# Attention values with the weights as the stationary operand and the sum as one more column

## The chip, the cores and the metric

The kernel runs on one core of one Trainium2 chip. The time is the device time of one execution in microseconds (us), the median of several. Most executions agree within 0.3%. A ratio is the mean time of one kernel's fast runs over that of the other's fast runs of the same rounds, so it is not quite the ratio of the medians quoted beside it.

The engines are called as in the profile: PE is TensorE (matmuls), PEld its weight loads, DVE VectorE, ACT ScalarE, POOL GpSimd (here mostly an issuer of transfers), SP the engine that issues the remaining transfers. L309 is line 309 of that kernel's source, so the same statement has other numbers in other kernels.

## The reference

Attention over keys that are also the values, pooled 4x4 from `kv` and projected, and then a two-layer block with a sigmoid GELU:

```python
kv_pool = kv.reshape(B, H//4, 4, W//4, 4, C).mean(axis=(2, 4))   # B=4, C=128, 768 keys a batch
k = v = kv_pool.reshape(B, -1, C) @ w_sr
s = (q @ k.transpose(0, 2, 1)) / sqrt(C)                          # 12288 queries a batch
a = exp(s - s.max()); a /= a.sum(-1) + 1e-9
x = a @ v
h = x @ w_in                                                      # 128 -> 2048
out = (h * sigmoid(1.702 * h)) @ w_out                            # 2048 -> 128
```

## The kernel before

Queries are taken in 96 groups of 512 tokens (a superset is four groups, a tile 128 tokens); the 768 keys are six chunks of 128. For three (group, chunk) pairs at a time TensorE makes scores, keys on the partitions and tokens on the columns, and ScalarE puts their exponentials in a ring `ag`. The values and sums are drained from the ring later, in an order fixed when the kernel is built: a small scheduler there keeps its own clock and decides what goes between the scores. PSUM's banks 6 and 7 are the two accumulators; the other six hold scores.

```python
def drain_attn(i, jc):                      # values: v stationary, 512 tokens moving
    if jc == 0:
        av_of[i] = acc(("av", i))
    nc.tensor.matmul(av_of[i], vs[b][:, jc, :], weights(("a", i, jc)),
                     start=(jc == 0), stop=(jc == JC - 1))
    if jc == JC - 1:                        # [cut] scale on the way out of PSUM
        nc.vector.tensor_tensor(xs[s][:, ...], av_of.pop(i), rb_of.pop(i), MUL)

def sums(s):                                # per superset: a column of ones times the weights
    ss = acc()
    for jc in range(JC):
        for gi in range(4):
            nc.tensor.matmul(ss[32*gi:32*gi+32, :], ones, weights(("a", 4*s+gi, jc)), ...)
    nc.vector.transpose(t1, ss); nc.vector.reciprocal(col, col); nc.vector.transpose(t2, t1)
    for gi in range(4):
        nc.gpsimd.partition_broadcast(rb, t2[32*gi:32*gi+1, :])

def background(i):                          # what is asked for beside group i
    if i % 4 == 0:
        load_qT(s + 2)                      # SP: transposing load of q for a superset
        cast_q(s + CAST)                    # POOL: q to bf16, HBM to HBM
    if i == 9:
        for jc in range(JC):
            load_chunk(1, jc)               # POOL: batch 1's keys, six casting loads
    # [cut] from group 15 on: pool_chunk, key_chunk, value_chunk of batch 1 on TensorE
```

Batches 2 and 3, which are needed much later, come otherwise: sixteen transfers each that add into SBUF (`add_kv`), then one add of two halves on DVE and transposes on TensorE.

The softmax here doesn't subtract the row's maximum and nothing guards it: scores larger than these inputs give would overflow.

## Time and profile before

| | before |
|---|---|
| time, median | 993.4 us |
| PE busy / ACT busy | 970.8 / 958.4 us of a span of 990.9 |
| DVE / POOL busy | 207.3 / 126.8 us |
| ACT's idle time before the exponentials | 19.6 us (all 196), 15.9 of it before the 188 of full size |

Both PE and ACT are near full. To see which one bounds, one counts each PE instruction at the distance between starts of its kind. That is done in the prediction, which also shows the lines. The same count is used below as "work", and the time from the first matmul to the end of the last less the work is called PE's idle time: 960.8 us of work and 24.4 us idle for the kernel before.

### The profile page before, as it was taken

The numbers are of one execution on the slowest core, as the hardware profiler recorded it, in microseconds if no ns is written. First come the engines' busy times: TensorE is split into PE (matmuls) and PEld (weight loads), VectorE is DVE, ScalarE is ACT, GpSimd is POOL, SyncE is SP. The second block draws the span as 40 slices with busy tenths as digits, with TensorE's granted clock in tenths as the row PEclk, the third lists the DMA queues.
The fourth block names the chain that finished last, engine by engine and source line by source line (L and its number), as shares of the span: only waits on it lengthen the run. The fifth ranks groups of instructions, "written<-read, shape, count | busy, mean of one in ns | idle before, by whom it ended". The sixth has DMA issues, their size and how long they took to land.

```text
span 990.9 us, 13081 instructions
## 1 busy us (share of the span) xinstructions
PE 970.8 (98%) x5041; PEld 438.7 (44%) x5135; DVE 207.3 (21%) x352; ACT 958.4 (97%) x713; POOL 126.8 (13%) x171
## 2 busy tenths in 40 slices
PE   7899999999999999999999999999999999999997
PEld 3444444444444444444444444444444444444443
DVE  4443334211110111101113333430110111011101
ACT  4999999999999999999999999999999999999997
POOL 3221322530133000000002222220000000000000
PEclk9999999999999999999999999999999999999999
DMA  9996941892399322222245520001222221222222
GB/s 182 166 210 113 120 86 33 97 158 43 74 150 173 60 37 41 35 41 43 41 77 97 112 59 22 1 1 32 43 36 40 43 43 33 43 44 39 36 43 43
DMA packets 273663, 69.10 MB, mean 70 GB/s; under 512 B 247552, under 2 KB 271232, under 8 KB 273280
## 3 DMA queue, kind: packets, MB, share of 16 engines
q0 software_dynamic: 29104, 32.51, 21.4%
q1 hardware_dynamic: 243440, 35.61, 21.2%
q8 instruction: 40, 0.66, 0.3%
q10 hardware_dynamic: 1056, 0.13, 0.1%
q14 instruction: 23, 0.19, 0.1%
HBM read 52.49 MB, written 35.65 MB: 89 GB/s over the span
## 4 chain that ended last, share of the span: by engine, by line
PE 87%; ACT 6%; DMA 4%; issue 1%; DVE 1%; POOL 0%; ACTq 0%; POOLq 0%
PE banks L389 31%; PE banks L382 31%; PE banks L312 11%; PE banks L304 11%; ACT ag L384 5%; DMA qT<-q_bf 4%; PE banks L327 3%; ACT ag L306 1%; DMA x<-in_q_dram 1%; DVE qT L209 1%; PE banks L203 0%; DVE o_sb L396 0%; PE banks L157 0%; POOL x L192 0%; PE banks L172 0%
## 5 line engine op out<-in xcount | busy, mean ns | idle before, releaser
L384 ACT ACTIVATE ag<-banks 128x1536 bf16<-128x1536 f32 x512 | 690.8, 1487 | 3.3 <-PE banks L382 2.7
L382 PE MATMUL banks<-x,w_in_sb 128*128 128x512 bf16 x1495 | 408.3, 379 | 1.1
L389 PE MATMUL banks<-ag,w_out_sb 128*128 128x512 bf16 x1510 | 405.3, 379 | 3.0 <-ACT ag L384 0.7
L306 ACT ACTIVATE ag<-banks 128x1536 bf16<-128x1536 f32 (+2 forms) x196 | 261.9, 1454 | 19.6 <-PE banks L304 19.6
L382 PEld LDWEIGHTS <-w_in_sb 128*128 128x128 bf16 x1536 | 149.7, 98 | 183.5 <-issue 6.5
L389 PEld LDWEIGHTS <-w_out_sb 128*128 128x128 bf16 x1536 | 150.0, 98 | 180.4 <-issue 0.8
L396 DVE STREAM_TRANSPOSE o_sb<-banks 128x512 f32<-128x512 f32 x96 | 68.8, 717 | 548.2 <-PE banks L389 521.1
L304 PE MATMUL banks<-qT,kT 128*128 128x512 bf16 x551 | 154.4, 379 | 8.1 <-ACT ag L306 4.5
L312 PE MATMUL banks<-ag,v 128*128 128x512 bf16 x574 | 155.4, 379 | 0.3
L338 POOL PARTITION_BROADCAST rb<-t x96 | 66.6, 797 | 425.7 <-DVE t L335 425.7
L319 DVE TENSOR_TENSOR x<-banks,rb 128x512 bf16<-128x512 f32 x96 | 66.4, 692 | 147.0 <-PE banks L312 124.5
L304 PEld LDWEIGHTS <-kT 128*128 128x128 bf16 x576 | 53.9, 97 | 78.2 <-issue 16.2
L312 PEld LDWEIGHTS <-v 128*128 128x128 bf16 x576 | 55.8, 98 | 66.7 <-issue 0.4
L146 POOL DMA_DIRECT2D kvs<-in_kv_dram x32 | 40.3, 1286 | 97.6 <-DMA kvs<-in_kv_dram 53.0
L327 PE MATMUL banks<-ag,ones 128*32 128x512 bf16 x576 | 35.5, 381 | 0.0
L331 DVE STREAM_TRANSPOSE t<-banks 128x512 f32<-128x512 f32 x24 | 17.2, 717 | 38.5 <-PE banks L327 38.5
L327 PEld LDWEIGHTS <-ones 128*32 128x32 bf16 x576 | 13.2, 96 | 20.6 <-issue 10.2
L335 DVE STREAM_TRANSPOSE t<-t 128x512 f32<-128x512 f32 x24 | 17.1, 711 | 1.0
L180 POOL DMA_DIRECT2D q_bf<-in_q_dram x20 | 10.9, 578 | 8.6 <-DMA x<-in_kv_dram 6.3
L209 DVE COPY qT<-banks 128x512 bf16<-128x512 bf16 x15 | 9.6, 686 | 3.7 <-PE banks L203 3.5
L250 PE MATMUL banks<-ones 128*32 128x512 bf16 x19 | 7.3, 513 | 0.9 <-DVE col L228 0.9
L123 PEld LDWEIGHTS <-x 128*128 128x128 bf16 x192 | 6.5, 96 | 3.0 <-DMA x<-in_kv_dram 0.5
(48 smaller groups left out, 82.4 us busy)
## 6 DMA issues: line engine op xcount, KB each, us to landing
out_dram<-o_sb SPq DMA_DIRECT2D x382, 64.0 KB, 1.9
kvs<-in_kv_dram POOLq DMA_DIRECT2D x32, 384.0 KB, 6.5
q_bf<-in_q_dram POOLq DMA_DIRECT2D x20, 512.0 KB, 7.5
x<-in_kv_dram POOLq DMA_DIRECT2D x12, 512.0 KB, 12.7
x<-in_q_dram POOLq DMA_DIRECT2D x3, 512.0 KB, 20.1
w_in_sb<-in_moe_w_in_dram POOLq DMA_DIRECT2D x1, 512.0 KB, 5.3
w_out_sb<-in_moe_w_out_dram POOLq DMA_DIRECT2D x1, 512.0 KB, 12.9
x<-in_q_dram POOLq DMA_DIRECT2D x1, 384.0 KB, 7.0
```

Source lines behind the costliest of these rows:

```text
L146: nc.gpsimd.dma_start(out=kv_sums[b][:, i2], in_=kv_p[b, i, w, :, i2], **({"accum_op": ADD} if n else {}))
L209: nc.vector.tensor_copy(dst, src)
L304: nc.tensor.matmul(ps[:, k, :], kTs[i // GB][:, jc * 128:(jc + 1) * 128], rhs, start=True, stop=True)
L306: nc.scalar.activation(place([("a",) + c for c in chunks]), ps, AF.Exp, scale=scale)
L312: nc.tensor.matmul(av_of[i], vs[b][:, jc, :], weights(("a", i, jc)), start=(jc == 0), stop=(jc == JC - 1))
L319: nc.vector.tensor_tensor(xs[s][:, (i % 4) * G:(i % 4 + 1) * G], av_of.pop(i), rb_of.pop(i), MUL)
L327: nc.tensor.matmul(ss[32 * gi:32 * gi + 32, :], ones, weights(("a", 4 * s + gi, jc)), start=(jc == 0), stop=(jc == JC - 1))
L338: nc.gpsimd.partition_broadcast(rb, t2[32 * gi:32 * gi + 1, :])
L382: nc.tensor.matmul(ps[:, k, :], w_in_sb[:, fc * 128:(fc + 1) * 128], xs[g // 4][:, (g % 4) * G:(g % 4 + 1) * G], start=True, stop=True)
L384: nc.scalar.activation(place([("m",) + c for c in chunks]), ps, AF.Gelu_apprx_sigmoid)
L389: nc.tensor.matmul(o_of[g], w_out_sb[:, fc, :], weights(("m", g, fc)), start=(fc == 0), stop=(fc == FCH - 1))
L396: nc.vector.transpose(o_sb, o_of.pop(g))
```

## The change

Its intent: with the weights stationary and the values moving, the result has tokens on the partitions. A 129th column of ones in the values then gives each token its sum beside its values, so that the block of sums, its two transposes on DVE and the four broadcasts on POOL fall away, and the scaling is by one number a partition. The price is four times as many weight loads, and six transposes on PE per six tiles, to bring the result back to tokens on columns.

```diff
-        nc.tensor.matmul(av_of[i], vs[b][:, jc, :], weights(("a", i, jc)), ...)
-    def sums(s): ...                                   # and its broadcasts
+    def drain_attn(t, a):                              # tile t of 128 tokens, half a of the chunks
+        for jc in range(a * K, a * K + K):
+            nc.tensor.matmul(av_of[u][:, k*(C+1):(k+1)*(C+1)], weights(("a", i, jc))[:, o:o+T],
+                             vs[i // GB][:, jc, 0:C+1], start=(jc == 0), stop=(jc == JC - 1))
+        if k == TS - 1 and a == 1:                     # three tiles fill an accumulator
+            nc.vector.reciprocal(rec, ps[:, :, C])
+            nc.vector.tensor_tensor(xt, ps[:, :, 0:C], rec.unsqueeze(2).broadcast_to(...), MUL)
+    def turn(w):                                       # six tiles back
+        for k in range(6):
+            nc.tensor.transpose(ps[:, k, :], xt[:, k, :], ident)
+        nc.vector.tensor_copy(x[:, o:o + 6 * T], ps)
 ... background(i):
-        if i == 9:
-            for jc in range(JC):
-                load_chunk(1, jc)
-        ... pool_chunk, key_chunk, value_chunk of batch 1
+        if i in ADDS:                                  # [4, 6, 8, 9, 11, 12, 14, 15]
+            add_kv(1, ADDS.index(i))                   # two accumulating transfers each
+        if i in (17, 19):
+            use_kv(1, (i - 17) // 2)                   # DVE adds halves, PE transposes
-    AG = 99
+    AG = 108
```

The last part is not in the title: batch 1's keys and values now come the way of batches 2 and 3. (The buffers are one tile `x`, and the scheduler's costs follow the new pieces.)

More of the change, by code (lines that the diff above doesn't have):

```diff
@@ L40 @@
     K = 3
+    T = 128
+    TS = 3
+    NT = B * N // T
     q_flat = q.rearrange("b n c -> (b n) c")
@@ L52 @@
     XS = NS // R
-    AG = 99
-    L = 10
+    AG = 108
     cpool = ctx.enter_context(tc.tile_pool(name="const", bufs=1))
@@ L62 @@
     agpool = ctx.enter_context(tc.tile_pool(name="ag", bufs=1))
-    npool = ctx.enter_context(tc.tile_pool(name="norm", bufs=5))
+    npool = ctx.enter_context(tc.tile_pool(name="norm", bufs=3))
     opool = ctx.enter_context(tc.tile_pool(name="op", bufs=3))
@@ L87, in acc_bf @@
     def acc_bf():
-        return acc()[:, 0:256].bitcast(BF)
+        return acc().bitcast(BF)
     def close(key, then):
@@ L93, in close @@
             free[m] = then
-    xs = {}
+    x = xpool.tile([128, XS * SG], BF, name="x")
     def x_tile(s):
-        return xpool.tile([128, SG], BF, name=f"x{s % XS}")
+        return x[:, s % XS * SG:(s % XS + 1) * SG]
     HC = H // 128
@@ L107, in new_keys @@
         kTs[b] = kvres.tile([128, J], BF, name="kT")
-        vs[b] = kvres.tile([128, JC, C], BF, name="v")
+        vs[b] = kvres.tile([128, JC, C + 2], BF, name="v")
+        nc.vector.memset(vs[b][:, :, C:C + 1], 1.0)
     def load_chunk(b, jc):
@@ L137, in value_chunk @@
         nc.tensor.matmul(ps[:, 0:128], pTs.pop((b, jc)), w_sr_sb, start=True, stop=True)
-        nc.vector.tensor_copy(vs[b][:, jc, :], ps[:, 0:128])
+        nc.vector.tensor_copy(vs[b][:, jc, 0:C], ps[:, 0:128])
     def add_kv(b, n):
@@ L173, in make_v @@
                              start=True, stop=True)
-        nc.vector.tensor_copy(vs[b][:, a * K:(a + 1) * K, :].rearrange("p k c -> p (k c)"), ps[:, :h])
+        nc.vector.tensor_copy(vs[b][:, a * K:(a + 1) * K, 0:C], ps[:, :h].rearrange("p (k c) -> p k c", k=K))
     qTs = {}
@@ L199, in transpose_q @@
             qTs[s] = qpool.tile([128, 1, SG], BF, name="qT")
-        ps = acc_bf().rearrange("p (i t) -> p i t", i=4)
+        ps = acc_bf()[:, 0:G].rearrange("p (i t) -> p i t", i=4)
         for i in range(4):
@@ L296, in weights @@
         return ag[:, slot_of[c], :]
-    rb_of, av_of = {}, {}
+    uses = {}
     def fill_attn(chunks, ps):
@@ L306, in fill_attn @@
         nc.scalar.activation(place([("a",) + c for c in chunks]), ps, AF.Exp, scale=scale)
-    def drain_attn(i, jc):
-        b, s = i // GB, i // 4
-        if jc == 0:
-            av_of[i] = acc(("av", i))
-        nc.tensor.matmul(av_of[i], vs[b][:, jc, :], weights(("a", i, jc)),
-                         start=(jc == 0), stop=(jc == JC - 1))
-        del slot_of["a", i, jc]
-        if jc == JC - 1:
-            close(("av", i), max(now, recip[i]) + EVACUATE)
-            if i % 4 == 0:
-                xs[s] = x_tile(s)
-            nc.vector.tensor_tensor(xs[s][:, (i % 4) * G:(i % 4 + 1) * G],
-                                    av_of.pop(i), rb_of.pop(i), MUL)
@@ L322, in sums @@
-    def sums(s):
-        ss = acc()
-        for jc in range(JC):
-            for gi in range(4):
-                nc.tensor.matmul(ss[32 * gi:32 * gi + 32, :], ones, weights(("a", 4 * s + gi, jc)),
-                                 start=(jc == 0), stop=(jc == JC - 1))
-        t1 = npool.tile([128, 512], F32, name="t1", bufs=1)
-        nc.vector.transpose(t1, ss)
-        col = t1.rearrange("p (m k) -> p m k", k=32)[:, :, 0]
-        nc.vector.reciprocal(col, col)
-        t2 = npool.tile([128, 512], F32, name="t2", bufs=1)
-        nc.vector.transpose(t2, t1)
-        for gi in range(4):
-            rb = npool.tile([128, 512], F32, name="rb")
-            nc.gpsimd.partition_broadcast(rb, t2[32 * gi:32 * gi + 1, :])
-            rb_of[4 * s + gi] = rb
+    def drain_attn(t, a):
+        i, u, k = t // 4, t // TS, t % TS
+        if k == a == 0:
+            av_of[u] = acc(("av", u))
+        o = t % 4 * T
+        for jc in range(a * K, a * K + K):
+            nc.tensor.matmul(av_of[u][:, k * (C + 1):(k + 1) * (C + 1)], weights(("a", i, jc))[:, o:o + T],
+                             vs[i // GB][:, jc, 0:C + 1], start=(jc == 0), stop=(jc == JC - 1))
+            if t % 4 == 3:
+                del slot_of["a", i, jc]
+        if k == TS - 1 and a == 1:
+            close(("av", u), now + EVACUATE)
+            ps = av_of.pop(u)[:, 0:TS * (C + 1)].rearrange("p (k c) -> p k c", k=TS)
+            rec = npool.tile([128, TS], F32, name="rec")
+            nc.vector.reciprocal(rec, ps[:, :, C])
+            if u % 2 == 0:
+                xt_of[u // 2] = npool.tile([128, 2 * TS, C], BF, name="xt")
+            nc.vector.tensor_tensor(xt_of[u // 2][:, u % 2 * TS:u % 2 * TS + TS, :], ps[:, :, 0:C],
+                                    rec.unsqueeze(2).broadcast_to([128, TS, C]), MUL)
+            if u % 2:
+                turns.append((now + TURN, u // 2))
@@ L341 @@
+    def turn(w):
+        n = 2 * TS
+        ps = acc_bf()[:, 0:n * T].rearrange("p (k t) -> p k t", k=n)
+        xt = xt_of.pop(w)
+        for k in range(n):
+            nc.tensor.transpose(ps[:, k, :], xt[:, k, :], ident)
+        o = w * n * T % (XS * SG)
+        nc.vector.tensor_copy(x[:, o:o + n * T], ps.rearrange("p k t -> p (k t)"))
+    av_of, xt_of, turns = {}, {}, []
+    ADDS = [4, 6, 8, 9, 11, 12, 14, 15]
     CAST = 5
@@ L350, in background @@
                 cast_q(s + CAST)
-        if i == 9:
-            for jc in range(JC):
-                load_chunk(1, jc)
-        if 0 <= i - 16 < JC:
-            extras.extend([(key_chunk, 1, i - 16), (value_chunk, 1, i - 16)])
-        if 0 <= i - 15 < JC:
-            extras.append((pool_chunk, 1, i - 15))
+        if i in ADDS:
+            add_kv(1, ADDS.index(i))
+        if i in (17, 19):
+            use_kv(1, (i - 17) // 2)
         if i == 26:
@@ L367, in background_moe, with use_kv @@
                 add_kv(b, g - lo)
-            a, n = divmod(g - lo - 9, 4)
-            if 0 <= a < 2:
-                if n == 0:
-                    sum_kv(b, a)
-                else:
-                    extras.append(((transpose_pooled, make_k, make_v)[n - 1], b, a))
+            if g in (lo + 9, lo + 13):
+                use_kv(b, (g - lo - 9) // 4)
+    def use_kv(b, a):
+        sum_kv(b, a)
+        extras.extend([(transpose_pooled, b, a), (make_k, b, a), (make_v, b, a)])
     extras = []
@@ L382, in fill_moe @@
             nc.tensor.matmul(ps[:, k, :], w_in_sb[:, fc * 128:(fc + 1) * 128],
-                             xs[g // 4][:, (g % 4) * G:(g % 4 + 1) * G], start=True, stop=True)
+                             x[:, g % (4 * XS) * G:(g % (4 * XS) + 1) * G], start=True, stop=True)
         nc.scalar.activation(place([("m",) + c for c in chunks]), ps, AF.Gelu_apprx_sigmoid)
@@ L415 @@
             part = part[m:]
-        todo += [("a", i, jc) for i in range(n * NG // R, (n + 1) * NG // R) for jc in range(JC)]
+        todo += [("a", t, a) for t in range(n * NT // R, (n + 1) * NT // R) for a in range(2)]
         flat = [(g, fc) for g in range(n * NG // R, (n + 1) * NG // R) for fc in range(FCH)]
@@ L420 @@
             seq.append(("m", flat[k:k + K]))
-    at, last_of = {}, {}
+    at = {}
     for p, (kind, part) in enumerate(seq):
@@ L425 @@
             at[(kind,) + c] = p
-            if kind == "a":
-                last_of[c[0] // 4] = p
+    for kind, t, a in [k for k in todo if k[0] == "a"]:
+        at["at", t, a] = max(at["a", t // 4, jc] for jc in range(a * K, a * K + K))
     begun = set()
     def prepare(p):
+        nonlocal now
         for f, *args in first.get(p, ()):
+            if f in COST:
+                now = max(now, free[next_acc()])
             f(*args)
+            if f in COST:
+                now += COST[f][0]
+                free[last_acc] = now + COST[f][1]
         kind, part = seq[p]
@@ L458 @@
         20: [(transpose_q, 14), (transpose_q, 15)]}
-    FIXED, CHUNK, SWITCH, HANDOVER, EVACUATE, LATE = 0.33, 1.975, 6.0, 1.0, 4.5, 4.5
+    FIXED, CHUNK, SWITCH, HANDOVER, EVACUATE, LATE = 0.33, 1.975, 6.0, 1.0, 4.5, 1.0
     COST = {pool_chunk: (2.5, 2.0), key_chunk: (0.7, 2.0), value_chunk: (0.7, 2.0),
-            transpose_pooled: (1.5, 3.0), make_k: (1.0, 3.0), make_v: (1.5, 3.0), sums: (8.0, 4.5)}
-    RECIP, SPREAD, AHEAD = 11.0, 3.7, 8.0
+            transpose_q: (1.2, 4.0),
+            transpose_pooled: (1.5, 3.0), make_k: (1.0, 3.0), make_v: (1.5, 3.0), turn: (1.5, 3.5)}
+    SMALL, TURN = 0.27, 5.5
     PAUSE = 4.0
     now, end, extra_at = 0.0, [], 0.0
-    recip = {}
-    done = done_s = drained_a = 0
+    done = 0
     def fill(p):
@@ L496 @@
             f = None
-            if done_s < NS and n >= last_of[done_s] and drained_a >= JC * (4 * done_s - 1):
-                if not any(k[0] == "av" for k in closes.values()):
-                    f, args = sums, (done_s,)
+            if turns and max(now, bank) >= turns[0][0]:
+                f, args = turn, turns[0][1:]
             if f is None and extras and now >= max(extra_at, bank):
                 f, *args = extras[0]
-            if f and max(now, bank) + COST[f][0] > limit + LATE and room >= 4 * K:
+            if f and max(now, bank) + COST[f][0] > limit + (LATE if f is turn else 3 * LATE) and room >= 4 * K:
                 f = None
@@ L508 @@
                 extra_at = now + PAUSE
-                if f is sums:
-                    for gi in range(4):
-                        recip[4 * done_s + gi] = now + RECIP + SPREAD * gi
-                    done_s += 1
+                if f is turn:
+                    turns.pop(0)
                 else:
@@ L518 @@
             kind, i, c = todo[done]
-            if at[todo[done]] > n or (kind == "a" and i >= 4 * done_s):
+            needs = at[("at" if kind == "a" else kind, i, c)]
+            cost = K * SMALL if kind == "a" else 1.0
+            if needs > n or (kind == "a" and i % TS == c == 0 and at["at", i + TS - 1, 1] > n):
                 break
-            start = max(now, end[at[todo[done]]] + HANDOVER)
-            if c == 0:
+            start = max(now, end[needs] + HANDOVER)
+            if c == 0 and (kind == "m" or i % TS == 0):
                 start = max(start, bank)
-                if kind == "a":
-                    start = max(start, recip[i] - AHEAD)
-            if start + 1.0 > limit and not (room < 2 * K + 1 or (room < 4 * K and start == now)):
+            if start + cost > limit and not (room < 2 * K + 1 or (room < 4 * K and start == now)):
                 break
-            now = start + 1.0
+            now = start + cost
             (drain_attn if kind == "a" else drain_moe)(i, c)
-            drained_a += kind == "a"
             done += 1
-    assert done == len(todo) and done_s == NS and not extras
+    assert done == len(todo) and not turns and not extras
 _INS = ['q', 'kv', 'w_sr', 'moe_w_in', 'moe_w_out']
```

## The prediction

> **What bounds the kernel now.** I read the busy table first, then the busy shares by slice, the groups by shape, windows of the timeline, and last the chain of waits. The busy table of the kernel before:
>
> ```profile
> PE 970.8 (98%) x5041; PEld 438.7 (44%) x5135; DVE 207.3 (21%) x352; ACT 958.4 (97%) x713; POOL 126.8 (13%) x171
> ```
>
> Two engines are full, so the question is which has slack. The groups by shape give the sizes:
>
> ```profile
> L384 ACT ACTIVATE ag<-banks 128x1536 bf16<-128x1536 f32 x512 | 690.8, 1487 | 3.3 <-PE banks L382 2.7 <-ACT ag L384 0.4
> L306 ACT ACTIVATE ag<-banks 128x1536 bf16<-128x1536 f32 x188 | 256.1, 1481 | 15.9 <-PE banks L304 15.8
> L312 PE MATMUL banks<-ag,v 128*128 128x512 bf16 x574 | 155.4, 379 | 0.3
> L327 PE MATMUL banks<-ag,ones 128*32 128x512 bf16 x576 | 35.5, 381 | 0.0
> L319 DVE TENSOR_TENSOR x<-banks,rb 128x512 bf16<-128x512 f32 x96 | 66.4, 692 | 147.0 <-PE banks L312 124.5 <-POOL rb L338 22.4
> ```
>
> A duration here includes pipeline latency; the rate is in the starts. In the timeline, three-matmul blocks of 512 columns start 0.65 us apart (215.6 ns each), and back-to-back activations end 1.343 us apart. ScalarE's floor is then about 704 x 1.343 = 945 us. TensorE's sum over all its instructions is: 3072 expert matmuls 662.3, 576 scores 124.2, 576 values 124.2, 24 blocks of sums 33.8 (1.41 each: the L327 block of 24 starts at 38.30, the next scores at 39.71), pooling 192 x 25 ns = 4.8, query transposes 64 x 55.5 ns = 3.6, the rest 8: 961 us. Counted window by window, this work leaves TensorE no idle time in nearly every window after 200 us. The chain agrees: PE 87%, ACT 6%. So TensorE is the bound, ScalarE is 16 us behind it, and a microsecond taken from TensorE is worth about one microsecond, until ScalarE's floor.
>
> DMA is the third resource. It is full in the first 37.5 us, and again when key/value sums are accumulated by DMA:
>
> ```profile
> 0.00:37.50 37.50, 29.07 (x242) 14.83 (x247) 18.05 (x54) 24.67 (x22) 9.14 (x19) 1.00 1.04 198
> 185.00:224.00 39.00, 38.84 (x180) 17.64 (x181) 6.68 (x11) 38.35 (x29) 17.07 (x15) 1.00 1.17 144
> ```
>
> (columns: stretch, its length, busy PE, PEld, DVE, ACT, POOL, granted clock, DMA share, GB/s). In the second stretch batch 2 is accumulated, two transfers a round:
>
> ```profile
> 195.69 1.32 POOL L146 DMA_DIRECT2D kvs<-in_kv_dram  x1 [2.84 <-DMA kvs<-in_kv_dram]
> 197.92 1.31 POOL L146 DMA_DIRECT2D kvs<-in_kv_dram  x1 [0.91 <-DMA kvs<-in_kv_dram]
> 201.49 1.31 POOL L146 DMA_DIRECT2D kvs<-in_kv_dram  x1 [2.26 <-DMA kvs<-in_kv_dram]
> 204.55 1.31 POOL L146 DMA_DIRECT2D kvs<-in_kv_dram  x1 [1.75 <-DMA kvs<-in_kv_dram]
> 208.93 1.31 POOL L146 DMA_DIRECT2D kvs<-in_kv_dram  x1 [3.07 <-DMA kvs<-in_kv_dram]
> ```
>
> Each transfer waits for its predecessor; a round takes 5.8 to 7.4 us.
>
> **What the Trainium skill says.** (1) "TensorE: Matmul & The Clock Gate", section "Back-to-back issue gap", gives a sustained stream of weight load plus 128-column matmul about 81 ns each, and an isolated gap of about 56 ns. This trace sides with 56: the query transposes, each with its own weights, start 55 to 56 ns apart, and the pooling matmuls (32 columns, own 128x128 weights) 25 ns. In the timeline:
>
> ```profile
> 9.49 0.62 PE L203 MATMUL banks<-ident,x 128*128 128x128 bf16 x8
> 12.40 0.56 PE L123 MATMUL banks<-sum,x 128*128 128x32 bf16 x16
> ```
>
> Less the 0.22 us latency of the last, 0.40 us for seven gaps is 57 ns. (2) "PSUM — Partial Sum Buffer", "Engine vs sequencer instructions": VectorE's queue is strict FIFO and matmuls start in program order. So a wait at the head of either holds up all that follows. (3) "DMA: Bandwidth & Descriptors", "Rules for kernel authors": an accumulating DMA must wait for the earlier DMA's semaphore to the same bytes. The rounds above do. (4) "TensorE: Matmul & The Clock Gate", "Why this matters for your kernels": idle gaps over about 3 us send TensorE back to its slow clock. Here the warm-up matmuls begin 427 ns apart and end at 216.
>
> **The change part by part.**
> TensorE, removed: sums, -33.8. Values: 2304 matmuls of 129 columns at an estimated 129/128 x 55.5 = 56 ns are 129.1 instead of 124.2, +4.9. Transposes back: 384 x 55.5 ns, +21.3. Batch 1's keys no longer pooled on TensorE: 96 x 25 ns, -2.4, and nearly nothing for its projections. Net -9.7: 951.5 us of work.
>
> VectorE: out go 24 x (0.717 + 0.256 + 0.711) = 40.4 and 96 x 0.692 = 66.4. In come 128 scalings of 384 f32 columns (a cast of 384 from PSUM took 558 ns), 128 small reciprocals (about 0.2, an estimate from the 256 ns of 16 columns) and 64 copies of 768 bf16 columns (about 0.56: the 384-column bf16 copy took 358 ns, of which some 160 fixed). 71 + 26 + 36 = 133 against 107. It stays near 25% busy, no bound. GpSimd loses its 96 broadcasts, 66.6 us that lay beside other work and are worth nothing.
>
> The half nobody sees in the title: batch 1's keys now come by accumulating DMA, 16 transfers in place of 6 plain ones. In the instruction order of the changed kernel these stand on GpSimd behind the start loads and three casts of q; the third cast was issued at 17.4 us and landed at 37.5. VectorE adds the two halves (waiting for the last transfers of the last round), and TensorE meets the transposes of that result after 105 score matmuls and 198 small value matmuls: 47.0 us of work. Before, the 105th score matmul came at 66 us with 48.1 us of work behind it, so the changed kernel arrives at about 65 us.
>
> When do the sums land? In saturated stretches of the batch-2 accumulation 310 packets a us moved, 768 a transfer: 2.5 us each. After 37.5: 16 x 2.5 = 40, two casts of q in the same queue 5, three transposing loads of q about 2.2 each at full rate, 6.6, and some 0.4 us of unfilled gap a round, 3: 54.6, so 92 us. Even with the adds alone it is 77.5. So TensorE, in order, stands from 65 until about 93 (0.65 us for VectorE's add), and ScalarE starves two steps later. This lies wholly on the path.
>
> From there: 904.5 us of TensorE work remain (951.5 - 47.0), about 5 us of idle (before, 913.1 us of work took 919 from that point, but 1 us of it waited for q, which the stall hides), 2 us of slow clock after the stall (estimate: 4 us at half rate). 93 + 904.5 + 5 + 2 = 1004.5. From the last matmul's end to the span's end it was 5 us, and timed runs are 2 to 3 us over the span: 1012.
>
> **The rivals.**
> (a) The stall is short or absent, because the sums land by 65 us. Then the -9.7 is nearly all kept: 984 us, still within 2%. For it: the schedule spreads the rounds as if 4.5 us each would do. Against: DMA is full until 37.5 us and 16 transfers take 40.
> (b) The small matmuls run at the skill's 81 ns: 2688 x 25 ns = +67 us, 1050 without and 1075 with a stall. Against: the 25 and 56 ns in this trace, though only in runs of up to 16.
> (c) The removed block of sums (1.41 us at a stretch, where two steps leave about 0.7 us of slack) starved ScalarE: 15.8 us of its idle time stands before the exponentials. Finer pieces mend that, but TensorE stays full, so I count it within the 9.7, not on top.
> (d) VectorE's evacuations hold the two accumulator banks: three tiles take about 1 us on TensorE spread over some 4 us, and 0.76 us on VectorE. I expect little.
>
> **Range and chances.** The landing at 92 may be 80 to 100, one for one in time: 1000 to 1020, and rival (a) pulls the lower end a little further. The limit of 2% is 1013.6, just above my value, so same and slower are near even. A gain over 2% would need the stall absent and ScalarE's idle time nearly gone: 4%.
>
> **What would show it.** Right: a hole in the slices of PE and ACT from about 65 to 93 us, with VectorE's add of the key/value halves waiting on DMA some 28 us; small value matmuls about 56 ns apart; PE full afterwards, and its work some 10 us less. Wrong: no hole there; or small matmuls at 70 ns and more; or repeated waits of TensorE for VectorE before value matmuls.

## The result, and the profile after

The changed kernel takes 1019.33 us (1018.52 to 1020.92, 4 runs) against 993.36 us (4 runs): a ratio of 1.0266, with an interval of 1.0248 to 1.0284. It is slower, in the way that the prediction gave as its main case, and by 7 us more than its middle value: that one lay just under the limit of 2%, the measured time lies above it and near the upper end of the range.

The busy table and the slices of the changed kernel (each digit is a fortieth of the span in tenths busy; the last row is PE's granted clock, the share of its full clock that it was given):

```profile
PE 961.4 (94%) x6461; PEld 525.2 (52%) x6579; DVE 228.1 (22%) x498; ACT 957.1 (94%) x713; POOL 79.3 (8%) x85
...
PE   7841999999999999999999999999999999999997
...
ACT  4950999999999999999999999999999999999996
...
PEclk9985999999999999999999999999999999999999
```

PE is 9 us less busy in a span that is 28 us longer. The third and fourth digits hold the difference: PE and ACT stand together. The timeline of PE shows where, and the list of waits (us in total, times, longest) names the cause:

```profile
63.27 0.51 PE L320 MATMUL banks<-v,ag 128*128 128x129 bf16 x6
99.13 0.50 PE L162 MATMUL banks<-ident,pooled 96*128 96x96 bf16 x4 [35.35 <-DVE pooled L157]
99.43 1.48 PE L309 MATMUL banks<-qT,kT 128*128 128x512 bf16 x3
```

```profile
PE banks L162 <- DVE pooled L157: 35.6, 2, 35.4
DVE pooled L157 <- DMA kvs<-in_kv_dram: 35.0, 1, 35.0
```

After six small value matmuls PE stands 35.35 us for DVE's add of the key halves (L157), and DVE stands 35.0 us for the last accumulating transfer. The scores that follow take 1.48 us for three, where three take 0.81 elsewhere: PE came back at half its clock (granted clock 0.50 from 99.1 to 103.9 us), and it kept that for 4.8 us.

The groups by shape that answer to those of before:

```profile
L388 ACT ACTIVATE ag<-banks 128x1536 bf16<-128x1536 f32 x512 | 690.6, 1474 | 0.2
...
L311 ACT ACTIVATE ag<-banks 128x1536 bf16<-128x1536 f32 x188 | 255.0, 1485 | 45.4 <-PE banks L309 45.0 <-PE banks L320 0.2
L320 PE MATMUL banks<-v,ag 128*128 128x129 bf16 x2304 | 173.8, 220 | 0.3 <-DVE x L344 0.3
...
L331 DVE TENSOR_TENSOR xt<-banks,rec 128x384 bf16<-128x384 f32 x128 | 71.3, 557 | 4.4
```

ACT's work is what it was; its idle time before the exponentials of full size went from 15.9 to 45.4 us, one wait of 36 us in it. The value matmuls almost never wait for DVE (0.3 us in all).

Counted by starts, PE's work is 955.7 us and its idle time 57.1. So the work fell by 5.1 us and the idle time rose by 32.7: the whole loss is idle time, and one hole holds it. The windows of the changed kernel (stretch, length, busy PE, PEld, DVE, ACT, POOL, clock, DMA share, GB/s) show what was busy in the hole:

```profile
0.00:37.50 37.50, 28.25 (x241) 14.54 (x246) 17.70 (x53) 24.25 (x22) 10.26 (x20) 1.00 1.03 197
...
64.00:99.00 35.00, 0.00 (x0) 0.00 (x0) 0.61 (x2) 0.98 (x1) 16.93 (x18) 0.53 1.18 149
...
185.00:224.00 39.00, 38.63 (x442) 29.06 (x447) 17.08 (x43) 38.97 (x30) 0.00 (x0) 1.00 0.11 15
```

Only DMA and its issuer worked between 64 and 99 us.

### The profile page after: what moved, and what is told of

It reads as the page before. It is cut to its first block, busy times and chain, and to the rows that moved or that the text cites. A ratio compares the mean times of both kernels' runs of the same rounds, so it can differ in the third digit from the quotient of the medians.

```text
span 1019.1 us, 15867 instructions
## 1 busy us (share of the span) xinstructions
PE 961.4 (94%) x6461; PEld 525.2 (52%) x6579; DVE 228.1 (22%) x498; ACT 957.1 (94%) x713; POOL 79.3 (8%) x85
## 4 chain that ended last, share of the span: by engine, by line
PE 85%; DMA 8%; ACT 3%; issue 2%; POOL 1%; DVE 1%; SPq 0%; POOLq 0%; DVEq 0%
PE banks L386 31%; PE banks L393 31%; PE banks L320 12%; PE banks L309 10%; DMA kvs<-in_kv_dram 6%; ACT ag L388 3%; PE banks L342 2%; DMA x<-in_kv_dram 2%; POOL kvs L151 0%; POOL x L197 0%; DMA out_dram<-o_sb 0%; POOL x L119 0%; DVE o_sb L400 0%; PE banks L162 0%; POOL q_bf L185 0%
## 5 line engine op out<-in xcount | busy, mean ns | idle before, releaser
L320 PEld LDWEIGHTS <-ag 128*128 128x128 bf16 x2304 | 152.2, 98 | 50.5 <-issue 2.3
L320 PE MATMUL banks<-v,ag 128*128 128x129 bf16 x2304 | 173.8, 220 | 0.3 <-DVE x L344 0.3
L151 POOL DMA_DIRECT2D kvs<-in_kv_dram x48 | 60.3, 1262 | 249.0 <-DMA kvs<-in_kv_dram 135.2
L331 DVE TENSOR_TENSOR xt<-banks,rec 128x384 bf16<-128x384 f32 x128 | 71.3, 557 | 4.4
L309 PEld LDWEIGHTS <-kT 128*128 128x128 bf16 x576 | 49.3, 97 | 34.5 <-issue 4.4
L344 DVE COPY x<-banks 128x768 bf16<-128x768 bf16 x64 | 35.6, 557 | 64.2 <-PE banks L342 64.2
L328 DVE RECIPROCAL rec<-banks 128x3 f32<-128x3 f32 x128 | 22.8, 178 | 97.4 <-PE banks L320 97.4
L162 PE MATMUL banks<-ident,pooled 96*128 96x96 bf16 x24 | 2.2, 217 | 35.6 <-DVE pooled L157 35.6
L342 PE MATMUL banks<-ident,xt 128*128 128x128 bf16 x384 | 31.8, 218 | 0.0
L342 PEld LDWEIGHTS <-xt 128*128 128x128 bf16 x384 | 24.8, 97 | 3.3
L157 DVE TENSOR_TENSOR pooled<-kvs 96x512 bf16<-96x512 f32 x6 | 3.9, 658 | 35.0 <-DMA kvs<-in_kv_dram 35.0
```

The lines of the kernel that those rows point to most:

```text
L151: nc.gpsimd.dma_start(out=kv_sums[b][:, i2], in_=kv_p[b, i, w, :, i2], **({"accum_op": ADD} if n else {}))
L309: nc.tensor.matmul(ps[:, k, :], kTs[i // GB][:, jc * 128:(jc + 1) * 128], rhs, start=True, stop=True)
L320: nc.tensor.matmul(av_of[u][:, k * (C + 1):(k + 1) * (C + 1)], weights(("a", i, jc))[:, o:o + T], vs[i // GB][:, jc, 0:C + 1], start=(jc = ...
L328: nc.vector.reciprocal(rec, ps[:, :, C])
L331: nc.vector.tensor_tensor(xt_of[u // 2][:, u % 2 * TS:u % 2 * TS + TS, :], ps[:, :, 0:C], rec.unsqueeze(2).broadcast_to([128, TS, C]), MUL)
L342: nc.tensor.transpose(ps[:, k, :], xt[:, k, :], ident)
```

## The experiments

All eleven kernels gave correct results. Each group was timed against the kernel before on the same chip. The expectations call the runs e1 to e11: e1 is the title's part alone, e2 the DMA part alone, e3 the keys asked for later, e4 the title's part with POOL paced (the "paced kernel"), e5 the transposes twice, e6 the rows of the values, e7 the scaling twice, e8 the same with the transposes later, e9 the kernel before with early loads, e10 the paced kernel without its first pacing copy, e11 the sums aligned too.

The theory after the result (A): the loss is the stand at batch 1's keys, and what the title names costs nothing or gains a little. The rival (B): the 2304 small matmuls with their weight loads, or the transposes, are the cost, and the hole merely covers it.

### The title's part alone

```diff
-        if i in ADDS:
-            add_kv(1, ADDS.index(i))
-        if i in (17, 19):
-            use_kv(1, (i - 17) // 2)
+        if i == 9:
+            for jc in range(JC):
+                load_chunk(1, jc)
+        if 0 <= i - 15 < JC:
+            extras.extend([(key_chunk, 1, i - 15), (value_chunk, 1, i - 15)])
+        if 0 <= i - 14 < JC:
+            extras.append((pool_chunk, 1, i - 14))
```

> The changed kernel with batch 1's keys and values brought in as in the kernel before (six plain casting loads, pooled on TensorE), the pooling one group earlier so that the order fits. Theory A (the whole loss is TensorE's stand of 35.4 us at the transposes of batch 1's pooled keys, caused by the accumulating transfers): the hole from 64 to 99 us is gone and the time is 984 to 989 us, a ratio of about 0.993 to before. Its small value matmuls start some 58 ns apart as in the changed kernel, so TensorE's work falls by only about 2 us; the rest of the gain comes from less idle time in the attention stages. Theory B (the 2304 weight loads and small matmuls, or the transposes back, are the loss): the time stays over 1005 us and TensorE is full.

Measured: 1006.28 us, ratio 1.0142 (1.0108 to 1.0176). Neither theory had this. The time is one that B allowed (over 1005 us), but B also asked for a full PE, and its work, counted by starts, is 2.8 us less than before; what grew is its idle time. The hole for the keys is gone, as A had it, and there is another one in its place. The timeline of PE, and then the DMA queues of this run between 44 and 64 us (packets, MB, share):

```profile
76.93 1.46 PE L309 MATMUL banks<-qT,kT 128*128 128x512 bf16 x3 [17.31 <-DMA qT<-q_bf]
```

```profile
q0 software_dynamic: 691, 4.17, 100.7%
q1 hardware_dynamic: 688, 0.18, 6.5%
```

PE stands 17.3 us for the first transposing load of q (with a second wait of 2.3 us later), and then runs at half its clock until 80.2 us. From issue to landing that load took 40.6 us here; in the kernel before and in the changed kernel it took 5.8. The reason can be read in the queues: POOL's casting transfers (q0) and SP's transposing load (q1) moved 691 and 688 packets, one for one (571 and 570, then 595 and 593, in two later runs with early loads), but a packet of q0 carries 6 KB on average and one of q1 262 bytes. While q0 always has a next packet, the transposing load gets a turn after each large packet and no more. The Trainium skill, "DMA: Bandwidth & Descriptors", section "Queues, rings and completion order", says that each DMA engine takes the queues in turn by packet; these counts agree.

And POOL kept q0 full because no broadcast holds it back any more. In the kernel before, its first broadcast stands in its order behind the first four casts and waits for DVE until 41.7 us; here it issued batch 1's loads from 23 us and further casts of q right behind them. That was my next theory (C): the broadcasts, which I had called worth nothing, had timed the transfers.

### The DMA part alone

```diff
 (the kernel before)
-        if i == 9: ... load_chunk(1, jc)      # and pool_chunk, key_chunk, value_chunk
+        if i in ADDS:                         # [cut] ADDS and use_kv as in the changed kernel
+            add_kv(1, ADDS.index(i))
+        if i in (17, 19):
+            use_kv(1, (i - 17) // 2)
```

> The kernel before with only batch 1's keys and values brought in by the accumulating transfers, as in the changed kernel; its sums and values stay as they were. Theory A: a hole of about 35 to 40 us on TensorE near 65 us, the time 1022 to 1035 us. Theory B: 990 to 996 us, no hole of more than a few us.

Measured: 1029.40 us, ratio 1.0357 (1.0335 to 1.0380). The time is as theory A had it, and B's 990 to 996 is out: the DMA part alone, with the old values and sums, costs 36 us. But there are three holes instead of one, 34.6 us together:

```profile
53.06 1.44 PE L312 MATMUL banks<-ag,v 128*128 128x512 bf16 x3 [7.20 <-DVE x L319]
...
83.31 1.44 PE L312 MATMUL banks<-ag,v 128*128 128x512 bf16 x3 [16.11 <-DVE x L319]
...
100.54 0.50 PE L157 MATMUL banks<-ident,pooled 96*128 96x96 bf16 x4 [11.28 <-DVE pooled L152]
```

The first two are waits for a broadcast (at 51.1 and 81.4 us) that stands in POOL's order behind accumulating transfers which wait for their predecessors; the third is the wait for the keys. So the transfers cost what theory A said, but in this kernel two thirds of it come by another path than the one it named.

### The keys asked for later

```diff
-        if i in (17, 19):
-            use_kv(1, (i - 17) // 2)
+        if i in (21, 22):
+            use_kv(1, i - 21)
```

> The changed kernel with VectorE's add of batch 1's halves and what follows asked for at groups 21 and 22 in place of 17 and 19: TensorE meets the transposes after 129 score matmuls and not 105, so some 10.9 us later, and no transfer is changed. Theory A: the sums still land near 98 us, the hole shrinks from 35 to about 24 us, and the time falls one for one to 1007 to 1010 us. Rival A2 (the stand holds up the issue of transfers too, so that the landing moves with it, or the late keys make new waits at group 24): less than 5 us gained, over 1014 us.

Measured: 1011.68 us (1008.45 to 1022.43), ratio 1.0201 (1.0139 to 1.0263). The runs scatter; the one with the profile took 1008.45 us, and in it the hole is as expected:

```profile
97.54 0.50 PE L162 MATMUL banks<-ident,pooled 96*128 96x96 bf16 x4 [23.82 <-DVE pooled L157]
```

PE stands from 73.7 to 97.5 us. The landing hardly moved (98.4 before, 96.8 here), so in this run the hole is the landing less the arrival. The median lies 1.7 us above the expected range. The rival (under 5 us gained, over 1014 us) fits the slowest run (1022.43), and that of 1014.18 lies at its border. These two had a lower granted clock over the whole run, 0.980 and 0.982 against 0.987 and 0.985, and the changed kernel with its hole of 35 us has 0.981 to 0.983; that points to longer stands, but these runs have no trace, so what lengthened them is open.

### The title's part, with POOL paced

```diff
 (the title's part alone)
             nc.vector.reciprocal(rec, ps[:, :, C])
+            if u == 0 or u * TS // 16 < (u + 1) * TS // 16:
+                seen = cpool.tile([128, 2], F32, name=f"seen{u}")
+                nc.vector.tensor_copy(seen[:, 0:1], rec[:, 0:1])
+                nc.gpsimd.tensor_copy(seen[:, 1:2], seen[:, 0:1])
```

POOL's copy waits for DVE, and the transfers behind it in POOL's order wait with it. No transfer is changed.

> The run with the title's part alone (e1), in which GpSimd now copies one column of a reciprocal from VectorE once after the first three tiles and once per superset, as a clock for its issue of transfers; no transfer is added or removed. Theory C (in e1 the hole of 17 us at 60 us came of the transposing load of q being starved by casting loads which GpSimd, rid of its broadcasts, issued 21 us too early): that load lands near 42 us again, no hole over 3 us is left, and the time is 984 to 991 us, ratio 0.992 to 0.998. Theory B (the small matmuls and transposes themselves cost the time): over 1000 us with TensorE full.

Measured: 985.22 us (985.12 to 985.45), ratio 0.9923 (0.9910 to 0.9935). Theory C's numbers hold, B's are out. Against the title's part alone this is 21.1 us, and the trace of that run accounts for it: 19.6 us of waiting for transposing loads, and 3.3 us at half the clock, which cost about 1.6.

```profile
PE 968.5 (99%) x6671; PEld 526.8 (54%) x6671; DVE 230.5 (23%) x533; ACT 957.6 (97%) x713; POOL 66.7 (7%) x100
```

The first transposing load landed 6.4 us after its issue. PE's work is 958.0 us and its idle time 19.0, against 960.8 and 24.4 before. So the title's idea (with the longer ring that it makes room for) gains 7.6 us in this form: 2.8 of work, and about 5 of idle time, from the attention stages: PE's idle time from 66 to 100, 100 to 200 and 500 to 690 us was 2.6, 1.5 and 2.8 before and is 0.7, 0.2 and 0.2 here. No run separates the longer ring from the smaller pieces of work, so which of them took away the idle time is not shown.

### Which engine the paced kernel waits for

Transposes twice:

```diff
         for k in range(n):
-            nc.tensor.transpose(ps[:, k, :], xt[:, k, :], ident)
+            for _ in range(2):
+                nc.tensor.transpose(ps[:, k, :], xt[:, k, :], ident)
```

> e4 with each transpose back done twice: 384 more at 55.5 ns, 21.3 us of TensorE. If TensorE is the bound over the whole span, the time rises by 18 to 22 us over e4. Rival: ScalarE is the bound by now and the transposes lie in TensorE's slack: a rise under 8 us.

Measured: 1006.57 us, 21.35 more than the paced kernel. Added to PE: 21.3. PE's idle time stayed at 19.3. So PE is the bound in the attention stages, where the transposes stand. For the stages in between this run says nothing: from 700 to 800 us of the paced kernel PE starts 463 matmuls, which at 215.6 ns are 99.8 us, and ACT's activations end 1.350 us apart from 700 to 970 against 1.343 back to back, so both are near full there.

Scaling twice:

```diff
-            nc.vector.tensor_tensor(xt, ps[:, :, 0:C], rec..., MUL)
+            for _ in range(2):
+                nc.vector.tensor_tensor(xt, ps[:, :, 0:C], rec..., MUL)
```

> e4 with VectorE's scaling of each accumulator done twice, 128 more of 0.557 us, 71 us of VectorE. If VectorE's evacuation is off the path, the time is that of e4 within 2 us; if the two accumulator banks wait for it, 5 us or more are lost and TensorE shows waits for VectorE before value matmuls.

Measured: 1005.04 us, 19.8 more. This was a surprise: DVE is busy for less than a third of the span even so (301 us). In the attention stages the share is higher, though not full. A window of the paced kernel and the same of this run (DVE is the third of the busy times):

```profile
115.00:175.00 60.00, 60.00 (x694) 44.93 (x692) 26.82 (x72) 59.13 (x44) 8.82 (x13) 1.00 0.50 74
115.00:175.00 60.00, 58.31 (x651) 42.61 (x650) 38.91 (x93) 57.46 (x43) 6.30 (x12) 1.00 0.46 71
```

That is 45% and 65%. PE's work is the same and its idle time 39.4 instead of 19.0. The waits of PE in this run:

```profile
PEld L347 <- issue: 14.4, 54, 0.5
...
PEld L320 <- issue: 5.0, 8, 1.0
...
PE banks L347 <- DVE xt L336: 3.1, 15, 0.4
PE banks L320 <- DVE xt L336: 3.0, 5, 0.9
```

Most are at the transposes (L347), a quarter of a microsecond at a time, before their weights `xt`, which are what DVE has just scaled. ("issue" means that the profile names no releaser; in the paced kernel the same weight loads had 2.6 us of idle time in all, so I put the rise down to `xt`.) I took this to be a matter of the fixed order (theory D) and moved the transposes back by as much as the second scaling takes:

```diff
-                turns.append((now + TURN, u // 2))
+                turns.append((now + TURN + 2.7, u // 2))
                 # [cut] batch 1 pooled one group earlier
```

> e7 (VectorE scales each accumulator twice) with the transposes back put 2.7 units of the kernel's own scheduling clock, about 0.6 us, later in TensorE's order, which is what the second scaling takes; batch 1 is pooled one group earlier so that the order still fits. Theory D (e7's 20 us came of TensorE standing at each of the 64 groups of transposes for a result that the fixed order expected sooner; VectorE's throughput is not the limit): at least 12 of the 20 us come back, 985 to 993 us. Rival D2 (VectorE is too slow for the two accumulator banks in the attention stages): within 5 us of e7, over 1000 us.

Measured: 1015.65 us, worse by 10.6 still. Theory D falls, and the number of D2 (within 5 us of e7) is not met either. The waits in this run:

```profile
PEld L320 <- issue: 16.3, 28, 1.0
PEld L347 <- issue: 14.7, 16, 1.0
...
PE banks L347 <- DVE xt L336: 10.2, 16, 0.7
PE banks L320 <- DVE xt L336: 10.0, 20, 0.8
```

Now the value matmuls (L320) wait for the scaling as well, 20 times 0.5 us, because, as I read it, the accumulator that they need next is the one that DVE is still reading. With two accumulators, and transposes that take one of them, moving the transposes then only moves the wait. What is shown: 0.56 us more for each of 128 accumulators, 71 us of DVE in all, cost 19.8 us, though DVE was idle for a third of these stages or more, so the time from the last value matmul of an accumulator to the end of DVE's scaling is partly on PE's path. It is 0.74 us in the paced kernel (0.178 + 0.557), which fits: PE's waits for it there are 0.4 us. That the two accumulators are the reason is argued; a third one was not tried.

### The rows of the values

In the changed kernel, starts of value matmuls are not evenly spaced: by chunk, 0 to 5, the next one starts after 56, 60, 59, 59, 56 and 60 ns. In a row of 130 bf16 elements per chunk these chunks start at 0, 260, 520, 780, 1040 and 1300 bytes.

```diff
-        vs[b] = kvres.tile([128, JC, C + 2], BF, name="v")
+        vs[b] = kvres.tile([128, JC, C + 32], BF, name="v")
```

> e4 with the rows of the values 160 elements apart in SBUF (320 bytes) in place of 130 (260 bytes). In the changed kernel value matmuls start 56 ns apart after chunks 0 and 4 of six and 59 to 60 ns after the others, which goes with the chunk and thus with the address of the moving operand. If alignment is the reason, all come to 56 ns and 2304 x 2.1 = 5 us are gained over e4. Rival: the spacing stays (it goes with the weights or the accumulator's address), and the time is that of e4 within 1 us.

Measured: 983.76 us, 1.5 less than the paced kernel; the ratio to before is 0.9908 (0.9895 to 0.9922). The intervals of the two ratios overlap, but no run of one kernel reaches the times of the other (983.2 to 984.5 and 985.1 to 985.5), so the 1.5 us are more than the rival's 1 and far less than the 5. All chunks are now at 57 ns (mean 56.7 against 58.2): 2304 x 1.5 = 3.5 us less work, of which 1.8 came back as idle time. So the spacing does go with the address of the moving rows (a row starts every 320 bytes in place of 260). Chunks 0 and 4, the fast ones before, are those that start at a multiple of 16 bytes from the first, and now all do; that fits, but no other distance was tried. The time gained is less than a third of what I expected, since only part of the spacing went and PE's idle time took up half of what went.

```diff
-            nc.tensor.matmul(av_of[u][:, k * (C + 1):(k + 1) * (C + 1)], ...
+            nc.tensor.matmul(av_of[u][:, k * 160:k * 160 + C + 1], ...     # [cut] and where it is read
```

> e6 with the three tiles of an accumulator 160 f32 columns apart in PSUM in place of 129. If the 57 ns that were left in e6 (against 55.5 of the transposes) come of the accumulator's address, the value matmuls come to about 56 ns and 2304 x 1 = 2 us are gained over e6's 983.8 us; if not, the time is that of e6 within 0.7 us.

Measured: 983.40 us (983.10 to 984.20), ratio 0.9901 (0.9885 to 0.9917). The spacing is 56.7 ns as before, so this shift of the accumulator's address plays no part. These two are the fastest kernels, 1% under the kernel before and alike within the scatter.

### Was it the early loads or the casts behind them?

In the kernel before, asking for batch 1's loads one group earlier puts them ahead of the first broadcast:

```diff
 (the kernel before)
-        if i == 9:
+        if i == 8:
             for jc in range(JC):
                 load_chunk(1, jc)
```

> The kernel before with one digit changed: batch 1's six casting loads are asked for at group 8 in place of 9, which puts them ahead of the first broadcast in GpSimd's order. Theory C (GpSimd's wait at its first broadcast is what keeps the DMA queue clear while the first transposing load of q runs): the loads are issued from 23 us, that load lands over 20 us late, TensorE stands some 15 to 20 us near 60 us, and the time is 1006 to 1014 us. Rival: the kernel before is insensitive to this, 991 to 996 us.

Measured: 992.72 us, ratio 0.9993 (0.9975 to 1.0011). The transfers did what theory C says: the loads went out from 23.1 us on, and the first transposing load took 23.6 us to land in place of 5.8. But it landed at 59.7 us, just when its first use came, and PE waited only 0.83 us for it. So the theory was right about the starving and wrong about its price; a second cause is needed for the hole of the title's part alone. After the early loads, the kernel before still has POOL wait at each later broadcast, so one cast followed at 44.3 us and the next at 56.8. In the title's part alone four casts, the load of `w_in`, two casts, the load of `w_out` and three more casts went out before 65 us, 1.8 to 3.3 us apart. To tell the two apart, the paced kernel without its first pacing copy:

```diff
 (the paced kernel)
-            if u == 0 or u * TS // 16 < (u + 1) * TS // 16:
+            if u * TS // 16 < (u + 1) * TS // 16:
```

> e4 without its first pacing copy: batch 1's six loads go out from 23 us as in e1 and in e9, but the later casts of q are still held back once per superset. Theory C2 (what made e1's hole was the run of later casts behind the early loads, which kept the software queue full until 77 us; the early loads alone starve the transposing load only until they are through, near 60 us, just when it is needed): that load lands at 58 to 63 us, TensorE stands 0 to 4 us, 985 to 990 us. Rival (the early loads themselves make the hole): 1000 us and more.

Measured: 991.41 us (990.46 to 992.25), ratio 0.9978 (0.9955 to 1.0001). With early loads and paced casts, the load took 27.3 us and landed at 63.9 us, a little later than expected (58 to 63), as the time is 1.4 us above the expected range. PE stood:

```profile
63.92 1.46 PE L309 MATMUL banks<-qT,kT 128*128 128x512 bf16 x3 [3.94 <-DMA qT<-q_bf]
```

That is 3.9 us where the flood of casts made 17.3, and the time is 6.2 us over the fully paced kernel and 15 under the unpaced one. (The 6.2 are the wait and 5.6 us at half the clock behind it, about 2.8.) So most of that hole came of the later casts, which this run holds back. What is left is not the early loads' alone: a cast that went out right behind them at 37.7 us, and one at 52.5, landed before the transposing load too.

## Why the prediction was right or wrong

**The bound.** "TensorE is the bound, ScalarE is 16 us behind it" held for work added in the attention stages: 21.3 us cost 21.35 us. For work taken away, "worth about one microsecond" held less well: the aligned rows took 3.5 us from PE and the time fell by 1.5.

**The stall.** The case it was built on came about: DVE's add waits for the last accumulating transfer, and PE stands behind it, in order. The landing was 98.3 us (predicted 92), and this is the term of the sum that was mis-sized. From the chain that ended last (start, length):

```profile
49.64 14.31 DMA kvs<-in_kv_dram
...
71.70 5.90 DMA kvs<-in_kv_dram
...
92.19 6.11 DMA kvs<-in_kv_dram
98.39 0.70 DVE pooled L157
```

The 16 transfers, two casts and three loads of q were given 54.6 us after 37.5, and took 60.8. The first two transfers landed at 40.6 us, 1.9 us earlier than the sum has it. The next six, with transposing loads and a cast beside them, took until 71.2 us: 30.6 us, where the sum allows 25.3 with all three loads counted here. The last eight, with one cast, took 27.1 us where it allows 24.1. The step that failed is "three transposing loads of q about 2.2 each at full rate": in the kernel before, the first such load kept the 16 DMA engines for 46.5% of the 8 us from 36 to 44 us, which is 3.7 us, and three at that rate are 4.5 us of the 8.3 that are missing. The rest is open; that a round which is held up also issues its next transfer later, so that gaps are longer than the 0.4 us allowed, is likely but not shown.

The arrival was 63.8 us (predicted 65), in part by luck. The 66 us from which it was worked out is the start of the 105th score matmul in the trace's records, of which eight before it are missing; by the weight loads, which are all there, the 105th came at 61.6 us. The prediction's own difference of 1.1 us would then have given 60.5. This does not touch the predicted time, since the landing sets when PE goes on. The hole was 35.4 us for a predicted 28.

**PE's work.** Predicted -9.7 us, measured -5.1. The term that was mis-sized is "an estimated 129/128 x 55.5 = 56 ns": the value matmuls start 58.2 ns apart on average, which makes 134.0 us of them and not 129.1. The transposes back (55.5 ns), the removed sums and the pooling were as counted.

**After the stall.** 904.5 us of work and 7 of idle time and slow clock were predicted. From 99.1 us to the end of the last matmul at 1013.8 it was 914.7 us: 904.5, plus 4.5 for the value matmuls that were left, plus 5.7. The half clock after the hole was there for 4.8 us (4 estimated). What the Trainium skill, "TensorE: Matmul & The Clock Gate", section "Why this matters for your kernels", says of idle gaps over about 3 us agrees, and the runs lie on both sides: after waits of 35.4, 17.3 and 3.9 us three scores took about 1.47 us in place of 0.81, after one of 2.3 us they took 0.82. A slip beside it: the warm-up matmuls end 226 ns apart, and 216 is the spacing of the later ones.

The sum for the profiled run (1020.9 us): 6.1 us later resumption, 4.5 us more work, 1.3 less idle and 0.4 less from the last matmul to the device time make 8.9 over 1012.

**VectorE.** Predicted 133 us for what comes in; measured 71.3 + 22.8 + 35.6 = 129.7. "I expect little" from the evacuations was right for this kernel (0.3 us of waits), but that DVE is "no bound" because it has room to spare was not: in the paced kernel half a microsecond more per accumulator costs 20 us.

**GpSimd.** That the broadcasts "lay beside other work and are worth nothing" is the sentence that the experiments correct. The broadcasts' own time is worth nothing. Their waits held back POOL's transfers, and with the old loading of batch 1 their removal costs 21 us where nothing takes their place (1006.3 against 985.2). In the changed kernel this did not show: its first transposing load took 5.8 us, and POOL stood 15.6 us before the accumulating transfer at 40.05.

**The rivals.** (a) said 984 us for no stall, and the paced kernel, which has none, takes 985.2. That the numbers are so near is luck: (a) had 9.7 us less work, and the paced kernel has 2.8 less work and 5 less idle time. (b) is out, with 56 to 60 ns on average for every chunk. (c), the finer pieces, may have been counted too low: in the paced kernel the idle time in the attention stages fell by some 5 us, beside the work, but the longer ring came with them. (d) is told above.

## What to carry to other kernels

A diff's title may not be its cost: look in the instruction order of every issuer for transfers that have become more, smaller or chained, work out when the last lands and when the in-order engines reach the instruction that needs it. When an instruction is removed from an engine that also issues transfers, ask what its wait was holding back, and pace the issue on purpose if something needed it. And an engine that is a quarter busy over the whole run, and less than half where it matters, can still have little slack in one place, where its latency stands between two uses of a scarce buffer.

## What the Trainium skill lacked or had wrong

- "TensorE: Matmul & The Clock Gate", section "Back-to-back issue gap": its sustained 81 ns for a weight load with a matmul of 128 columns is not what these runs show. Transposes with their own weights started 55.5 ns apart, 2304 value matmuls of 129 columns 56 to 60, so the isolated formula's 56 is nearer. No page that I read has the effect of the moving rows' address: 58.2 ns with rows every 260 bytes, 56.7 with rows every 320.
- The same page, section "Part 4: PE-mode transpose", gives about 275 ns for a transpose in a kernel. The duration here is 218 ns, but what a kernel pays is the distance of starts, 55.5 ns (21.35 us for 384).
- "DMA: Bandwidth & Descriptors", section "Queues, rings and completion order", gives the turn by packet but not what it does to a queue of small packets: 691 against 688 packets, 4.17 against 0.18 MB, and a transposing load that took 40.6 us instead of 5.8.
- No page that I read gives the pace of chained accumulating transfers: here 3.1 us each for 384 KB at the end (the last four), and 5.1 with transposing loads and a cast among them (six).
